# First chunk of x loaded in three pieces over two DMA queues, and recorded instruction orders in place of a greedy planner

## The chip, the cores and the metric

The kernel runs on one core of a Trainium2 chip. TensorE (PE) does the matmuls, VectorE (DVE), ScalarE (ACT) and GpSimd (POOL) the elementwise work, SyncE (SP) issues almost all DMAs. The metric is the device time of one execution in microseconds, as the median of several runs. Where the profile is used, its time is that of one profiled execution: the span runs from its first to its last instruction, and the execution's own time is a little longer.

## The reference

Two blocks read the same x (2048 tokens of 512) and are mixed by a gate per token. Cut to what matters:

```python
g = sigmoid((x * gate_w).sum(-1, keepdims=True))
# A: attention with a memory, 32 heads of 16, four segments of 512 tokens
q, k, v = x @ wq, x @ wk, x @ wv
for s in range(4):
    p = softmax(qs @ ks.T * 0.25 + causal_mask)      # inside the segment
    a_mem = (phi(qs) @ M) / (phi(qs) @ z + 1e-6)     # memory of earlier segments
    o = sigmoid(beta) * a_mem + (1 - sigmoid(beta)) * (p @ vs)
    M, z = M + phi(ks).T @ vs, z + phi(ks).sum(tokens)
a = concat(o) @ wo
# B: gated feed-forward, 1792 wide
b = (relu(x @ W_gate) * (x @ W_up)) @ W_down
out = g * a + (1 - g) * b
```

phi(t) is t + 1 where t > 0 and exp(t) elsewhere.

## The kernel before, in words

**Work.** The tokens go through in four chunks, which are also the four segments. Each chunk needs, on TensorE: the projections q, k and v (`proj`, lines 790 and 792, 48 matmuls of 128 x 128 by 512 columns); 18 *quads* of scores (`visit`, line 912), each filling four PSUM banks with 32-row matmuls that run four at a time; four *PV* products (line 968), one for each group G of eight heads, of 64 x 17 tiles; the memory update `mu` (line 835) and read-out `nd` (line 855); the feed-forward products with W_gate and W_up (`ffn`, line 1042, four matmuls for each of 28 products); and the output tiles (`outp`), which add the product with wo (line 1074, four matmuls) to that with W_down (line 1081, fourteen). Full 128-row matmuls, quads, PV and mu are different kinds of work for the array (modes f, r, h, c in the code).

ScalarE turns each quad into exponentials with one instruction over 2048 columns (line 928); GpSimd cuts the causal triangle out of them (line 934), 256 times in all; PV reads the result and VectorE transposes and scales it (lines 978 to 997). Other PSUM results are copied out by VectorE or ScalarE.

**The opening.** TensorE needs x with its features on the partitions. For chunk 0, `load` (line 618) brings x in as two halves of 256 tokens ("hT" is their buffer), SP issues both, and TensorE transposes them with an identity matrix: sixteen matmuls of 128 columns (line 706), eight evacuations called xc (line 713). Until x is there, eleven matmuls on a constant (`warm`, line 692: five of 512 columns, six of 128) keep TensorE running. Then come all four columns of Q, feature slice by feature slice, all of K, and V. Later chunks are transposed by the DMA (line 620). The three "touch" loads of 1 KB and the dummy exponential `tab` (line 645), which brings ScalarE's table load, are all that ScalarE's queue has at the start. VectorE zeroes the PSUM banks 4 to 7 (line 684), and every product that opens a bank is made to wait for that.

**What sets the order.** All work is added as `Op`s with their reads and writes. `Sched` then plays a cost model forward: at each step it takes, for each engine, the best ready head of some priority queues, with release times (`after`), bank rules and seeded jitter (`_choose`, `ready`, `_bank_choice`), and places the earliest. `place` writes the waits on semaphores and books a duration. What comes out is a fixed program for each engine: on the chip each engine goes through its list in order, and an instruction that has to wait holds up all that stand behind it on its engine, DMA issues on SP among them. Quads always use the banks 0 to 3, everything else what is free.

```python
x0 = A_x[0, 0:512, :].rearrange("(h p i) d -> h p i d", h=2, i=2)
for h in range(2):
    load("sp", [f"hT{2 * h}", f"hT{2 * h + 1}"], V.hT[:, 2 * h:2 * h + 2, :], x0[h], 1 << 18)
...
xps, xcs = [warm(5, 512, 0, 3), warm(6, 128, 0, 3)], {"dve": [], "act": []}
...
rdy = [h for h in heads if h[1] <= now + 20.0]
if rdy:
    best = min(rdy, key=lambda h: (h[0], h[1] + self.jitter(h[2])))
    return best[2], best[1]
```

Of the kernel before, what the change touches and what calls it, by code (L numbers as in the profile page):

```python
# [2 lines left out]

# [13 lines left out]
LAG = 0  # L17
PAIR = 1
LASTK = 17
HWAIT = 250.0  # L20
HEARLY = 3500.0
MWAIT = 500.0
PVR = 2
NEXT = 1150.0
TNN = 2
STRICT = 6000.0
PE_LAT = 175.0
SWITCH = 106.0
GATE_T = {0: 20000.0, 1: 44000.0, 2: 90000.0, 3: 140000.0}
UNIT_T = 400.0  # L30
X1_T = 19000.0
X2_T = 34000.0
H1_T = 14000.0
LX = 300.0
DCOST = {"ldwg0_0": 1000.0, "ldbraw": 1800.0, "ldgwb": 1300.0, "ldx1_0": 1500.0, "vsh0": 1100.0, "vsh1": 1100.0, "vsh2": 1100.0, "vsh3": 1100.0}
LAND0 = {"ldhT0": 2850.0, "ldhT2": 3100.0, "ldwq0": 3150.0, "ldwq1": 3200.0, "ldwq2": 3100.0, "ldwq3": 3000.0}
NBLK = 36
QTN, EKN, HTN, OTN, XR = 8, 4, 19, 8, 3
SBX = 0
LOW_T = {"main": 0.0, "att": 3000.0, "proj": 2000.0, "ffn": 2000.0, "mid": 3000.0, "out": 5000.0}  # L40
WIN = 8000.0
EVAC_P = 0.5
ND_P = 0.2
ADP = 1
TSP = 0
OAP = 0
UNITS = [[8] * 18] * 4
ORDER = [[(0, 1, 7, 2, 6, 3, 5, 4), (4, 0, 1, 7, 2, 6, 3, 5)] * 2] * 4
# [30 lines left out]
class Epoch:  # L79
    _n = 0  # L80

    def __init__(self, cls="mid", nb=1, at=None):
        self.nb = nb
        self.at = at
        self.group = (self,)
        Epoch._n += 1
        self.res = f"ACCep{Epoch._n}"
        self.bank = None
        self.readers = []
        self.cls = cls  # L90


class Op:
    __slots__ = ("engs", "eng", "fns", "occs", "lat", "reads", "writes", "name", "dma", "nbytes", "mode", "ep", "role",
                 "after", "nbk", "port", "base", "preds", "stream", "idx", "start", "end", "done", "cidx", "gate", "nd", "mates")

    def __init__(self, alts, reads=(), writes=(), name="", lat=0.0, dma=False, nbytes=0, mode="f", ep=None, role=None):
# [13 lines left out]
        self.after = 0.0  # L111
        self.nbk = 2
        self.port = name.startswith(PORT)
        self.base = None
        self.preds = []
        self.gate = None
        self.mates = ()
# [11 lines left out]
class Sched:  # L129
    ENGS = ("pe", "act", "dve", "pool", "sp")  # L130
    CAPS = {"ffn": 3, "proj": 2, "mid": 2, "out": 2}

    def __init__(self, ndma=16, nbanks=8, seeds=(0,)):
        self.seeds = seeds
        self.jit = {}
        self.knobs = {}
        self.low_from = False
        self.mates = ()
# [9 lines left out]
        self.queues = {e: [] for e in self.ENGS}  # L148
        self.dma_rr = 0
        self.port_free = 0.0  # L150
        self.relax = False
# [7 lines left out]
        self.busy = {e: 0.0 for e in self.ENGS}  # L159
        self.ops = []  # L160
        self.log = []
# [8 lines left out]
    def add(self, op):  # L170
# [42 lines left out]
        self.ops.append(op)  # L213
        return op

    def queue(self, prio, ops):
        by = {}
        for t in ops:
            for e in t.engs:
                by.setdefault(e, []).append(t)  # L220
        for e, ts in by.items():
            self.queues[e].append([prio, ts, 0])

    def _bank_free(self, prev, e):
        if prev is None:
            return 0.0
        return max((r.end + LAT for r in prev.readers if self.know[e][r.stream] < r.idx), default=0.0)

    def pv_due(self):
        q = self.queues["pe"][self.pvq]  # L230
        while q[2] < len(q[1]) and q[1][q[2]].done:
            q[2] += 1
        if q[2] >= len(q[1]) or q[1][q[2]].gate is None:
            return 0
        t = self.now["pe"] + 500.0
        return (PVR if q[1][q[2]].mates else q[1][q[2]].nbk) if all(p.done and p.end <= t for p, _ in q[1][q[2]].preds) else 0

    def next_visit(self):
        q = self.queues["pe"][self.attq]
        while q[2] < len(q[1]) and q[1][q[2]].done:  # L240
            q[2] += 1
        return q[1][q[2]] if q[2] < len(q[1]) else None

    def visit_in(self, dt):
        op = self.next_visit()
        if op is None:
            return False
        t = self.now["pe"] + dt
        if op.after > t or not all(p.done and p.end <= t for p, _ in op.preds):
            return False  # L250
        return all(p.done and p.end <= t + 700.0 for g in op.ep.group for rd in g.readers for p, _ in rd.preds if p.ep not in op.ep.group and p.cidx < op.cidx)

    def soon(self, dt):
        op = self.next_visit()
        if op is None or op.after - HEARLY > self.now["pe"] + dt:
            return False
        if not all(p.done and p.end + LAT <= self.now["pe"] + dt for p, _ in op.preds):
            return False
        t = max((self._bank_free(x, "pe") if x is None or all(r.done for r in x.readers) else 1e9) for x in self.bank_ep[:4])
        return t <= self.now["pe"] + dt  # L260

    def next_sides(self):
        op = self.next_visit()
        return 0 if op is None else len(op.ep.group) - 1

    def low(self, cls):
        return 0 if self.low_from and (self.relax or not self.visit_in(LOW_T[cls])) else 4

    def _bank_choice(self, ep, e, taken=()):
        cls, nb, n = ep.cls, ep.nb, len(self.bank_ep)  # L270
        idle = [i not in taken and (p is None or all(r.done for r in p.readers)) for i, p in enumerate(self.bank_ep)]
        if ep.at is not None:
            own = range(ep.at, ep.at + nb)
            return (ep.at, max(self._bank_free(self.bank_ep[i], e) for i in own)) if all(idle[i] for i in own) else None
        lo = 4 if cls == "side" else self.low(cls)
        if cls in ("proj", "ffn", "mid", "out"):
            held = sum(not f and p.cls == cls for f, p in zip(idle, self.bank_ep))
            if held + nb > (self.knob()[3] if cls == "ffn" else 2):
                return None
            free = sum(idle[lo:])  # L280
            if (free - nb < max(self.pv_due(), 1) if nb == 1 else free < (2 if self.relax else 3)):
                return None
            room = sum(idle[4:]) - (self.next_sides() if self.visit_in(self.knob()[1]) and not self.relax else 0)
        else:
            room = 8
        best = None
        for bi in range(lo, n - nb + 1):
            if not all(idle[bi:bi + nb]) or bi + nb > 4 and min(nb, bi + nb - 4) > room:
                continue
            ft = max(self._bank_free(p, e) for p in self.bank_ep[bi:bi + nb])  # L290
            key = ft + (300.0 if bi < 4 else 0.0)
            if nb == 1:
                key += 0.0 if not idle[bi ^ 1] else 200.0
            if best is None or key < best[2]:
                best = (bi, ft, key)
        return best and best[:2]

    def _banks(self, op, e):
        taken, out, t = set(), [], 0.0
        for ep in op.ep.group:  # L300
            bc = self._bank_choice(ep, e, taken)
            if bc is None:
                return None
# [11 lines left out]
    def ready(self, op, e):  # L315
        t0 = self.now[e]
        t = op.after - (HEARLY if op.mode == "r" and self.mode == "h" else 0.0)
        if op.gate is not None:
# [10 lines left out]
            if len(ft) < op.nbk:  # L329
                return None  # L330
# [871 lines left out]
```

## Time and profile before

| | us |
|---|---|
| median of 3 runs | 263.42 |
| lowest and highest of them | 262.78, 263.67 |
| the profiled execution's own time | 263.54 |
| its span | 262.3 |

| engine | busy us | share of the span |
|---|---|---|
| TensorE matmul | 255.7 | 97% |
| ScalarE | 184.5 | 70% |
| VectorE | 179.5 | 68% |
| GpSimd | 130.7 | 50% |

A busy share is a sum over instructions. Matmuls overlap in the array and the ends of single matmuls are modelled, so distances between starts tell more than durations. Some matmul records are missing: line 1042 has 432 of its 448 matmuls in the profile. In the timeline a row is a start, a length, an engine, a line, an operation with its tiles, and the number of instructions; brackets give the idle time ahead of it and what ended it. "issue" means that nothing the profile shows was waited for.

### The profile page before, as it was taken

To read this page: it belongs to the slowest core of one execution; us is meant where nothing else is said; L and a number is where in the kernel's file an instruction comes from. 1 tells how busy PE (TensorE), PEld (TensorE's weight loads), DVE (VectorE), ACT (ScalarE), POOL (GpSimd) and SP (SyncE) were. 2 spreads that over 40 slices of the span, in tenths; PEclk is the share of its full clock that TensorE was granted. 3 is DMA by queue.
4 is the path that set the end of the run, shared out by engine and by line. 5 is a ranking of instruction groups with operands and counts; after the bars stand their busy time and mean duration, and the time that the engine had idled before them with its cause. 6 is when DMAs were issued, how large, how long until landed. Compare 5 with 4: busy or idle time off the path is not lost.

```text
span 262.3 us, 6420 instructions
## 1 busy us (share of the span) xinstructions
PE 255.7 (97%) x2619; PEld 114.7 (44%) x2653; DVE 179.5 (68%) x356; ACT 184.5 (70%) x160; POOL 130.7 (50%) x295
## 2 busy tenths in 40 slices
PE   8999999999999999999999999999999999999997
PEld 5444443444344544434444544444444444444444
DVE  5488878788986577778788577757667716467600
ACT  4586689999789779785778687677777665576021
POOL 3036557564646457666645457846364454545100
PEclk9999999999999999999999999999999999999999
DMA  6999746930261135212040232010132100100011
GB/s 200 290 308 249 162 63 135 287 46 22 66 143 40 24 74 109 62 23 24 19 107 7 56 96 27 2 41 2 22 82 43 23 21 22 40 2 2 0 42 40
DMA packets 34925, 19.87 MB, mean 76 GB/s; under 512 B 24016, under 2 KB 34128, under 8 KB 34896
## 3 DMA queue, kind: packets, MB, share of 16 engines
q1 hardware_dynamic: 34800, 19.46, 31.6%
q8 instruction: 21, 0.34, 0.6%
q14 instruction: 8, 0.07, 0.1%
q10 hardware_dynamic: 96, 0.00, 0.0%
HBM read 10.40 MB, written 2.11 MB: 48 GB/s over the span
## 4 chain that ended last, share of the span: by engine, by line
PE 97%; issue 1%; DVE 1%
PE ps L1042 38%; PE ps L1081 19%; PE ps L792 11%; PE ps L912 9%; PE ps L968 6%; PE ps L790 5%; PE ps L1074 5%; PE ps L855 1%; PE ps L692 1%; PE ps L706 1%; PE ps L835 0%; DVE hT L1053 0%; DVE Tn L978 0%; DVE osb L745 0%; DVE osb L1090 0%
## 5 line engine op out<-in xcount | busy, mean ns | idle before, releaser
L934 POOL TENSOR_SCALAR_AFFINE_SELECT E<-E 64x256 bf16<-64x256 bf16 (+1 forms) x256 | 110.3, 442 | 112.2 <-ACT E L928 82.9
L928 ACT ACTIVATE E<-ps 128x2048 bf16<-128x2048 f32 x72 | 135.1, 1876 | 38.7 <-PE ps L912 38.6
L1042 PE MATMUL ps<-xT,wu 128*128 128x512 bf16 x213 | 57.2, 380 | 1.4 <-issue 1.3
L1042 PE MATMUL ps<-xT,wg 128*128 128x512 bf16 x219 | 57.7, 380 | 0.6 <-issue 0.3
L1081 PE MATMUL ps<-wd,hT 128*128 128x512 bf16 (+2 forms) x229 | 52.8, 367 | 0.9 <-issue 0.6
L1053 DVE TENSOR_TENSOR hT<-ps,rl 128x512 bf16<-128x512 f32 x56 | 38.5, 687 | 16.6 <-PE ps L1042 16.4
L1081 PEld LDWEIGHTS ps<-wd,hT 128*128 128x128 bf16 x238 | 21.4, 98 | 23.8 <-issue 2.4
L1042 PEld LDWEIGHTS ps<-xT,wg 128*128 128x128 bf16 x224 | 20.6, 98 | 25.7 <-issue 2.8
L1042 PEld LDWEIGHTS ps<-xT,wu 128*128 128x128 bf16 x224 | 20.1, 98 | 25.4 <-issue 3.5
L912 PE MATMUL ps<-qT,kp 32*128 32x192 bf16 (+7 forms) x512 | 28.6, 287 | 0.0
L978 DVE STREAM_TRANSPOSE Tn<-ps 128x512 f32<-128x512 f32 x32 | 21.3, 696 | 8.7 <-PE ps L968 8.7
L1051 DVE TENSOR_SCALAR rl<-ps 128x512 bf16<-128x512 f32 x30 | 20.7, 690 | 8.5 <-PE ps L1042 8.2
L1090 DVE TENSOR_SCALAR osb<-ps,omg 128x512 bf16<-128x512 f32 (+1 forms) x8 | 5.6, 701 | 26.0 <-PE ps L1081 15.1
L1050 ACT ACTIVATE rl<-ps 128x512 bf16<-128x512 f32 x26 | 15.5, 598 | 10.0 <-PE ps L1042 9.7
L912 PEld LDWEIGHTS ps<-qT,kp 32*128 32x128 bf16 x512 | 8.2, 92 | 25.3 <-issue 13.1
L968 PE MATMUL ps<-E,vaug 64*17 64x128 bf16 (+7 forms) x512 | 18.7, 283 | 0.0
L968 PE MATMUL ps<-E,vsh 64*17 64x128 bf16 (+7 forms) x512 | 18.3, 283 | 0.0
L1091 ACT ACTIVATE osb<-ps,omg 128x512 bf16<-128x512 f32 (+1 forms) x9 | 6.1, 674 | 16.4 <-PE ps L1074 14.0
L792 PE MATMUL ps<-xT,wq 128*128 128x512 bf16 x61 | 16.0, 390 | 0.4 <-issue 0.3
L1074 PE MATMUL ps<-wo,oT 128*128 128x512 bf16 (+2 forms) x67 | 16.2, 366 | 0.2 <-issue 0.2
L792 PE MATMUL ps<-xT,wk 128*128 128x512 bf16 x60 | 15.6, 380 | 0.4 <-issue 0.3
L968 PEld LDWEIGHTS ps<-E,vaug 64*17 64x17 bf16 x512 | 11.6, 86 | 8.5 <-issue 4.4
(68 smaller groups left out, 233.6 us busy)
## 6 DMA issues: line engine op xcount, KB each, us to landing
vsh<-vaug SPq DMA_DIRECT2D x8, 272.0 KB, 4.2
osb<-in_A_x_dram SPq DMA_DIRECT2D x16, 128.0 KB, 2.3
out_dram<-osb SPq DMA_DIRECT2D x15, 128.0 KB, 1.7
wg<-in_B_W_gate_dram SPq DMA_DIRECT2D x8, 224.0 KB, 5.7
wu<-in_B_W_up_dram SPq DMA_DIRECT2D x8, 224.0 KB, 6.2
wd<-in_B_W_down_dram SPq DMA_DIRECT2D x1, 1792.0 KB, 10.6
hT<-in_A_x_dram SPq DMA_DIRECT2D x2, 256.0 KB, 2.9
wq<-in_A_wq_dram SPq DMA_DIRECT2D x4, 128.0 KB, 3.5
```

Source lines behind the costliest of these rows:

```text
L792: ins = e.matmul(A(ep)[:, :], lhsT=w[:, kt, col * 128:(col + 1) * 128], rhs=V.xT[:, kt, tok:tok + 512], start=(kt == 0), stop=(kt == KT - 1))
L912: ins = q.matmul(dst, lhsT=V.kp[r, kslot(s, G), c, :], rhs=V.qT[r, qslot(s, G), q0:q0 + w], start=True, stop=True, tile_position=(32 * jj, ...
L928: acts.append(act(lambda a: a.activation(V.E[:, base * 512:base * 512 + min(2048, 4 * W)], PF[:, 0:min(2048, 4 * W)], ACT.Exp, scale=SCALE ...
L934: pools.append(pool(lambda g, ap=ap, lim=lim, pat=pat: g.affine_select(out=ap, in_=ap, compare_op=ALU.is_ge, fill=0.0, base=lim, pattern=[ ...
L968: ins = q.matmul(A(eps[p])[32 * jj:32 * jj + 17, 64 * (c + u):64 * (c + u + n)], lhsT=v[:, 8 * G + 2 * jj + p, :], rhs=V.E[r, f:f + 64 * n ...
L978: ds.append(dve(lambda e, p=p, ep=eps[p]: e.transpose(V.Tn[:, 2 * (G % (TNN // 2)) + p, :], A(ep)[:, :]), t_dve(512), writes=[f"Tn{2 * (G ...
L1042: ins = e.matmul(A(ep)[:, :], lhsT=w[:, kt, f * 128:(f + 1) * 128], rhs=V.xT[:, kt, c % XR * 512:(c % XR + 1) * 512], start=(kt == 0), sto ...
L1050: evs.append(sc.add(Op([("act", lambda e, ep=eg, r=r: e.activation(V.rl[:, r, :], A(ep)[:, :], ACT.Relu), t_act(512)), ("dve", lambda e, e ...
L1051: ("dve", lambda e, ep=eg, r=r: e.tensor_scalar(V.rl[:, r, :], A(ep)[:, :], 0.0, None, ALU.max), t_dve(512))],
L1053: evs.append(dve(lambda e, ep=eu, r=r, hs=hs: e.tensor_tensor(V.hT[:, hs, :], A(ep)[:, :], V.rl[:, r, :], ALU.mult), t_dve(512), reads=[f" ...
L1074: ins = e.matmul(A(ep)[:, 0:c1 - c0], lhsT=V.oT[:, ot[G], i * 128:(i + 1) * 128], rhs=V.wo[:, G, c0:c1], start=st_ and G == 0, stop=sp_ an ...
L1081: ins = e.matmul(A(ep)[:, 0:c1 - c0], lhsT=V.hT[:, slots[f], i * 128:(i + 1) * 128], rhs=V.wd[:, f, c0:c1], start=st_ and f == f0, stop=sp ...
```

## The change

1. Chunk 0 of x comes in three loads: tokens 0 to 127 ("hT0") on SP, 128 to 255 ("hT1") on ScalarE's queue, 256 to 511 ("hT2", "hT3") on SP. The sixteen transposing matmuls stay sixteen; four evacuations now cover two feature slices of 128 tokens (xca0, xca1, xcb0, xcb1), four cover one slice of 256 tokens as before (xc4 to xc7).
2. The first tile of wq is issued on ScalarE's queue too. That queue's order becomes hT1, wq0, the three touches, then the dummy exponential.
3. The second warm-up group has four matmuls in place of six. The zeroing of PSUM and the waits on it are gone.
4. Priority queues, release times, jitter and bank rules are gone. Each engine's order is a recorded list of numbers (`ORDER`), and each PSUM result's bank a digit of `BANKS`; an `Op`'s number is its place in the order in which `program` adds them. `run` and `place` remain, so that waits are worked out as before. A quad may start at any bank from 0 to 4.
5. `visit` can split quads over several visits (`SEVEN`); the lists that would ask for it are empty, so there are 72 visits of one quad, as before.
6. In the recorded order chunk 0 starts with the columns 2 and 0 of Q only, then all of K and a part of V; the columns 1 and 3 of Q come after the first quad.

The core of the diff, with the first entries of the lists:

```diff
+LAND0 = {"ldhT0": 2650.0, "ldhT1": 2750.0, "ldhT2": 3050.0, "ldwq0": 3500.0, "ldwq1": 3500.0, "ldwq2": 3400.0, "ldwq3": 3550.0, "ldwk0": 3450.0, "ldwk1": 3400.0, "ldwk2": 3350.0, "ldwk3": 3400.0,
+SEVEN = [(), (), (), ()]
+ORDER = {k: [int(x) for x in v.split()] for k, v in {
+    "pe": """
+58 59 60 62 64 66 68 70 72 74 159 134 160 135 161 162 136 137 149 139 174 140 164 150 175 165 190 196 191 193 385 194 144 391 145 392 386 202 187 146
...
+    "act": """
+5 7 0 1 2 3 63 67 71 75 151 154 197 179 395 203 148 76 209 186 215 413 189 221 227 425 238 341 244 335 90 250 336 256 344 351 449 273 354 279 360 285
...
+    "sp": """
+4 6 8 9 10 11 12 13 14 15 16 17 18 19 20 21 22 23 24 25 26 28 29 39 27 82 84 43 30 158 38 86 32 36 40 37 88 201 200 31 34 33 95 183 45 182 35 157 97
...
     def run(self):
+        for ep in self.eps:
+            if ep.at is None:
+                ep.bank = int(self.banks[ep.idx])
...
+        todo = {e: [self.ops[i] for i in self.order[e]] for e in self.ENGS}
...
-    x0 = A_x[0, 0:512, :].rearrange("(h p i) d -> h p i d", h=2, i=2)
-    for h in range(2):
-        load("sp", [f"hT{2 * h}", f"hT{2 * h + 1}"], V.hT[:, 2 * h:2 * h + 2, :], x0[h], 1 << 18)
+    for n, w in enumerate((W_g, W_u, W_d)):
+        load("act", [f"touch{n}"], V.adT[0:16, 32 * n:32 * n + 32], w[0:16, 0:32], 1024)
+    act(lambda e: e.activation(V.eb[:, 0:8], nc.const_aps.tensor(1.0, [128, 8], BF16), ACT.Exp), 100, writes=["eb"], name="tab")
+    load("sp", ["hT0"], V.hT[:, 0, :], A_x[0, 0:128, :], 1 << 17)
+    load("act", ["hT1"], V.hT[:, 1, :], A_x[0, 128:256, :], 1 << 17)
+    load("sp", ["hT2", "hT3"], V.hT[:, 2:4, :], A_x[0, 256:512, :].rearrange("(p i) d -> p i d", i=2), 1 << 18)
...
-            load(eng, [f"{nm}{kt}"], w[:, kt, :], src[kt * 128:(kt + 1) * 128, :], 1 << 17)
+            load("act" if (nm, kt) == ("wq", 0) else eng, [f"{nm}{kt}"], w[:, kt, :], src[kt * 128:(kt + 1) * 128, :], 1 << 17)
...
-    for b in range(4):
-        ds.append(dve(lambda e, b=b: e.memset(PS[:, 4 + b, :], 0.0), 500, writes=[f"init{b}"], name=f"init{b}"))
...
+    for m, n, role in ((5, 512, "w"), (4, 128, "w2")):
```

In these numbers 0 to 2 are the touches, 3 is `tab`, 4 to 6 the loads of x, 7 to 18 those of wq, wk and wv, 58 and 59 the warm-ups, 60 to 75 transposes and evacuations by turns, 134 to 195 the projections of chunk 0 (134 to 137 column 0 of Q, 159 to 162 column 2), and 196 the first quad.

More of the change, by code (lines that the diff above doesn't have):

```diff
@@ L213, in add @@
         self.ops.append(op)
-        return op
[L216 to L296, printed above, removed]
```

710 lines of the change are left out of this document (235 added, 475 removed), and 35 rows, old and new, of the table ORDER.

## The prediction

> **What bounds the kernel now.** First the page: how busy each engine is, and what the chain that ended last consists of.
>
> ```profile
> span 262.3 us, 6420 instructions
> ...
> PE 255.7 (97%) x2619; PEld 114.7 (44%) x2653; DVE 179.5 (68%) x356; ACT 184.5 (70%) x160; POOL 130.7 (50%) x295
> ...
> PE 97%; issue 1%; DVE 1%
> ```
>
> The chain is TensorE from end to end. A busy share alone does not say that nothing is lost between the matmuls, so the second view is TensorE's waits after its first transpose, window 3.8 to 260.4 (us in total, times, longest):
>
> ```profile
> PE ps L1042 <- issue: 1.6, 10, 0.2
> PE ps L1081 <- issue: 0.6, 4, 0.2
> PE ps L792 <- issue: 0.6, 4, 0.2
> PE ps L1074 <- issue: 0.2, 1, 0.2
> PE ps L1042 <- DVE Tn L978: 0.2, 1, 0.2
> ```
>
> 3.2 us in twenty pieces, none over 0.2. The third view, TensorE's timeline, says what such a piece is:
>
> ```profile
> 15.57 0.40 PE L912 MATMUL ps<-qT,kp 32*128 32x448 bf16 x8
> 15.90 1.47 PE L790 MATMUL ps<-wv,xT 128*128 128x512 bf16 x6
> ...
> 18.07 1.03 PE L1042 MATMUL ps<-xT,wu 128*128 128x512 bf16 x4
> 19.03 0.40 PE L912 MATMUL ps<-qT,kp 32*128 32x384 bf16 x8
> 19.59 0.81 PE L1042 MATMUL ps<-xT,wg 128*128 128x512 bf16 x3 [0.16 <-issue]
> 20.23 1.03 PE L1042 MATMUL ps<-xT,wu 128*128 128x512 bf16 x4
> ```
>
> Three matmuls from 19.59 to 20.23 are 0.214 us each. The quad (scores, L912) at 15.57 is followed after 0.33 us, the one at 19.03 after 0.56; but L1042 issues four matmuls per product, and only three are recorded. The "wait" is one unrecorded matmul (0.33 + 0.21). Four matmuls from 18.07 fill 0.86 of 0.96 us: entering a quad costs 0.10. So TensorE has no hole that a better order could fill; an order can change only how often it changes kind of work, the opening, and the end.
>
> The fourth view is the opening's timeline:
>
> ```profile
> 0.80 1.28 ACT L645 ACT_TABLE_LOAD   x1 [0.80 <-PEq L1187]
> 0.81 0.86 SPq L618 DMA_DIRECT2D hT<-in_A_x_dram  x2
> 0.84 2.93 PE L692 MATMUL ps<-const-bfloat16-1.0 128*128 128x512 bf16 x11 [0.84 <-PEq L1187]
> 0.87 0.39 ACTq L618 DMA_DIRECT2D adT<-in_B_W_gate_dram  x1
> 1.72 1.85 SPq L618 DMA_DIRECT2D wq<-in_A_wq_dram  x4
> 2.10 0.21 ACT L645 ACTIVATE eb<-const-bfloat16-1.0 128x8 f32<-128x8 bf16 x1
> 3.61 1.86 SPq L618 DMA_DIRECT2D wk<-in_A_wk_dram  x4
> 3.74 1.63 PEld L706 LDWEIGHTS ps<-ident,hT 128*128 128x128 bf16 x16 [0.23 <-DMA hT<-in_A_x_dram]
> 5.42 4.17 PE L792 MATMUL ps<-xT,wq 128*128 128x512 bf16 x16
> 5.85 0.15 PEld L792 LDWEIGHTS ps<-xT,wq 128*128 128x128 bf16 x1 [0.28 <-issue]
> 6.28 0.15 PEld L792 LDWEIGHTS ps<-xT,wq 128*128 128x128 bf16 x1 [0.28 <-issue]
> 6.63 2.47 PEld L792 LDWEIGHTS ps<-xT,wq 128*128 128x128 bf16 x12 [0.20 <-issue]
> 7.41 1.86 SPq L618 DMA_DIRECT2D wg<-in_B_W_gate_dram  x4
> ```
>
> Eleven warm-up matmuls cover the wait for x; the transposes start at 3.74, when x has landed, and Q at 5.42. The first Q matmuls come 0.43 us apart, the rest 0.21: TensorE runs at half pace until about 6.5 us, though the granted clock reads 1.00 all along.
>
> **The change, part by part.**
>
> *First chunk of x.* What the start waits for is the landing:
>
> ```profile
> vsh<-vaug SPq DMA_DIRECT2D x8, 272.0 KB, 4.2
> osb<-in_A_x_dram SPq DMA_DIRECT2D x16, 128.0 KB, 2.3
> ...
> hT<-in_A_x_dram SPq DMA_DIRECT2D x2, 256.0 KB, 2.9
> wq<-in_A_wq_dram SPq DMA_DIRECT2D x4, 128.0 KB, 3.5
> wk<-in_A_wk_dram SPq DMA_DIRECT2D x4, 128.0 KB, 3.2
> ```
>
> Today 0.81 + 2.9 = 3.71. The new first load has half the bytes. If it lands no sooner, the gain is 0. The quiet 128 KB row (2.3) would land it at 3.11, but the warm-ups end later: five of 512 columns at 0.43 and four of 128 at a quarter of that, 2.57 us from 0.84, so 3.41, and 3.74 - 3.41 = 0.33 is the most to be gained. I take the middle, 0.17: transposes from 3.57, Q from 3.57 + (5.42 - 3.74) = 5.25. The second slice (ACT, about 0.87 + 2.9 = 3.77) is wanted after four transposes at 3.57 + 4 x 0.105 = 3.99 (sixteen take 5.42 - 3.74), the 256 KB rest (SP, 1.24 + 2.9 = 4.14) after eight, at 4.41; cover 0.2 to 0.3.
>
> What is the earlier start worth? At half pace until 6.5, 0.17 us does half its work: 0.09. If the pace changed earlier by as much, all 0.17. I take 0.09, since the first warm-up still starts at 0.84.
>
> [...]
>
> *ScalarE's queue.* The groups by line give the evacuations of the transposes, and the PSUM memsets used below:
>
> ```profile
> L684 DVE MEMSET ps<- 128x512 f32 x4 | 1.9, 485 | 1.2 <-PEq L1187 1.0
> L713 DVE CAST xT<-ps 128x256 bf16<-128x256 f32 x4 | 1.5, 420 | 1.2 <-PE ps L706 1.2
> L713 ACT ACTIVATE xT<-ps 128x256 bf16<-128x256 f32 x4 | 1.4, 382 | 2.3 <-PE ps L706 2.3
> ```
>
> Five DMA issues now precede the dummy exponential; at SP's 0.43 each (0.86 for two) they end at 0.87 + 5 x 0.43 = 3.02. If the table load (1.28) waits for them, ScalarE is free at 3.02 + 1.28 + 0.21 = 4.51 instead of 2.31. Behind it stand four copies of 0.38: xca1, xcb1, xc5, xc7, done at 4.89, 5.27, 5.65 and 6.03. Q now does columns 2 and 0 alone, so each slice of x is used after two matmuls instead of four: the second at 5.25 + 0.86 = 6.11 (needs xc5: cover 0.4), the last slice near 7.0 (needs xc7: 0.9). Cost 0; if the cover fails, each 0.1 of lateness costs 0.1, or half before 6.5.
>
> *Weights.* wq0 goes to ACT, and SP issues all that follows 0.47 us earlier (a fourth of 1.86), so K's deadline moves against its loads. Eight Q matmuls, three of them slow, end at 5.25 + 3 x 0.43 + 5 x 0.216 = 7.6 (today, by the same count, sixteen end at 9.5). wk0 and wk1 are issued at 3.14 and 3.6 and land 3.2 later, 6.8; wk2, wk3 by 7.8, wanted after three half products at 8.9. Eight K halves (3.45) and one V half bring the first quad to about 11.6. The first wg product comes at about 12.8, where its loads matter:
>
> ```profile
> wg<-in_B_W_gate_dram SPq DMA_DIRECT2D x2, 224.0 KB, 4.2
> ```
>
> The first two issued at 7.41 and 7.9 land at 11.6 and 12.1 today, at or before that after the change: cover 0.7 at least. Cost 0.
>
> *Further down SP's queue* one placed wait matters: the vsh copies wait for the last V copy, ScalarE's vcp0_1, which the table puts behind exp0_0_3 and a relu, by my count of its products near 25 us. Behind them on SP stand wg1_2, wu1_1, wu1_0. At 4.2 us for vsh the shifted values land at 29.3; the table puts the first PV near 32. The next user, wg0_7, is near 35. Cost 0.
>
> *PSUM.* Four VectorE memsets (485 ns each) go from the very start; VectorE's first copies had to wait 1.2 us for the transposes all the same. Worth 0. Quads may now stand at banks 0 to 4; the exponential reads four banks in one piece as before. Cost 0.
>
> *Orders.* Counted in program() order, the "pe" table holds the same products, 72 quads, 16 PV and 3 mu, with two warm-ups less. Its changes of kind number 164, 60 of them from full matmuls into a quad. The before timeline also has 164 and 60. At 0.10 each, a difference of 0. With no wait to remove, all reordering after 12 us is worth 0 at best; a misplaced entry costs its lateness.
>
> *End.* The table keeps the last 128 columns' fourteen matmuls, the wo product, VectorE's copy and the 32 KB store last. Cost 0.
>
> Sum: -0.09 against the profiled 263.54 (span 262.3 and 1.2 around it), which lies 0.12 above the median: 263.42 - 0.09 = 263.33, say **263.3**.
>
> **The rivals.**
>
> *No earlier landing* (two queues share engines): 263.4. For it, loads in company land late: 128 KB of wq take 3.5 us, 256 KB of x ahead of them 2.9. Against it, the first slice is issued 0.06 ahead of the second.
>
> *Full pace sooner.* The change of pace at 6.5 falls on no event of the program. If it comes up to 2.7 us sooner, at the first transpose, up to 2.72/2 = 1.4 is saved: 262.0 to 263; I price it at 262.4. The three runs of before spread over 0.9 us, which would fit such a shift between runs; nothing shows that the change causes it. [...]
>
> *Slower: a hole ahead of the transposes.* Warm-ups now end at 3.41 against 3.63 today. If x lands at 3.57 to 3.74, TensorE idles 0.2 to 0.3, today 0.1. If the half-pace stretch, 6.5 - 0.84 = 5.7 us from the first matmul, starts anew there, it lasts to 3.57 + 5.7 = 9.3, and 2.8 us more at half pace cost 1.4: 264.7. It decides from the point where a hole of 0.2, not 0.1, counts as idleness. Against it: small holes are common in any opening.
>
> *Slower by the tables.* Replayed orders cannot step aside: if one quad in ten of the 72 waits 0.15 us, they lose 7 x 0.15 = 1.1: 264.4. Against it: before's program is as fixed once built, and never waits.
>
> **How the numbers follow.** Forecast 0.55, no earlier landing 0.15, full pace sooner 0.14, hole 0.09, tables 0.07. A measurement of this kernel tells 0.3%, 0.8 us, from no change: faster means under 262.6, slower over 264.2. Faster 0.14, same 0.70, slower 0.16. The range must leave out 0.2: the slower cases (0.16) and the outer part of full pace sooner, so 262.2 to 263.9; the unknown landing (0 to 0.33) and the opening's cover lie inside.
>
> **What would show it.** Right: transposes at 3.45 to 3.7, first quad near 11.6, no TensorE wait over 0.2 after that, the last matmul about as long before the end. Wrong: Q rows 0.43 apart beyond 7 us (hole), under three slow ones (full pace sooner), a wait on ACT's xT copies or on a wg load (cover gone), or quads with real gaps ahead of them (tables).

## The result, and the profile after

The changed kernel takes 264.34 us (median of 7 runs, 263.90 to 264.92) against 263.22 for the kernel before in the same measurement (7 runs, 262.78 to 263.67): ratio 1.0047, interval 1.0032 to 1.0063. It is slower by 1.1 us, where 0.1 us less was forecast. Of the kernels tried further down, pad_both_wq0_late had one execution, the profiled one, at a mean granted clock of 0.987 (268.88 us); it is left out of that kernel's median, and its columns in the table are empty.

The page of the changed kernel's profile (its own time 264.91, span 263.3) shows TensorE busy as before, and a chain that is no longer TensorE alone:

```profile
span 263.3 us, 6429 instructions
PE 259.1 (98%) x2651; PEld 113.7 (43%) x2651; DVE 173.9 (66%) x346; ACT 187.0 (71%) x166; POOL 120.6 (46%) x295
...
PE 94%; DMA 3%; DVE 1%; SPq 0%; issue 0%
```

TensorE's waits between 3.3 and 260 us (in total, times, longest) name three places; none of them is among the waits of before:

```profile
PE ps L852 <- DVE oT L763: 0.5, 1, 0.5
PE ps L523 <- DMA hT<-in_A_x_dram: 0.4, 1, 0.4
PE ps L583 <- DVE xT L507: 0.2, 1, 0.2
```

Two of them lie in the opening. TensorE's rows of the timeline:

```profile
3.55 1.04 PE L514 MATMUL ps<-ident,hT 128*128 128x128 bf16 x8
4.97 0.62 PE L523 MATMUL ps<-ident,hT 128*128 128x128 bf16 x8 [0.39 <-DMA hT<-in_A_x_dram]
5.77 1.90 PE L583 MATMUL ps<-xT,wq 128*128 128x512 bf16 x8 [0.18 <-DVE xT L507]
7.51 3.62 PE L583 MATMUL ps<-xT,wk 128*128 128x512 bf16 x16
10.96 0.59 PE L581 MATMUL ps<-wv,xT 128*128 128x512 bf16 x2
11.49 0.39 PE L696 MATMUL ps<-qT,kp 32*128 32x512 bf16 x4
```

The transposes start at 3.55 and the first quad at 11.49 (it was 12.55), both as forecast. In between stands a hole that was not: the second eight transposes wait for the third piece of x until 4.97. That piece was issued in the SP group that starts at 0.81, behind the first, so at about 1.24; it took 3.7 us. What paid for the hole is the pace: the eight Q matmuls from 5.77 to 7.51 go at 0.22 us each, so the full pace was there at 5.8 and not at 6.5.

The third place is the first product with wo, at 82.75. The rows that lead to it, in the timeline of all engines:

```profile
75.84 3.06 SPq L543 DMA_DIRECT2D osb<-in_A_x_dram  x1
...
81.37 0.69 DVE L544 CUSTOM_DVE_ANT_0 osb<-osb,gwb 128x512 bf16<-128x512 bf16 x1 [1.82 <-DMA osb<-in_A_x_dram]
...
81.98 0.71 DVE L763 STREAM_TRANSPOSE oT<-adT 128x512 bf16<-128x512 bf16 x1
...
82.75 0.82 PE L852 MATMUL ps<-wo,oT 128*128 128x512 bf16 x3 [0.47 <-DVE oT L763]
```

A tile of x for the gate, issued at 75.84, keeps SP for 3.06 us and lands 5.5 us after its issue; VectorE stands idle 1.82 us for it, though the transpose of oT behind it in VectorE's list needs nothing from it; TensorE then waits for oT. In the same stretch lies a 16 KB packet of kind "instruction" on a queue of its own, q8, which took 2.93 us from 75.7 on (this trace's others take 0.9 to 1.4). The trace has 21 of these to TensorE's 5302 matmuls and weight loads, one to about 250; from that they are taken here for fetches of TensorE's program, and the 8 KB packets of the same kind on q14 for those of the other engines. From 75.5 to 79 us the packet is 5.2% of the 16 DMA engines' time, which is one engine for 2.93 us:

```profile
q8 instruction: 1, 0.02, 5.2%
...
osb<-in_A_x_dram SPq DMA_DIRECT2D x1, 128.0 KB, 5.5
```

Last, the end: first before's timeline and its DMA view of the window 261 to 263.4 (packets, MB and the share of 16 engines; then the issues, with the time to landing), then the same of the changed kernel.

```profile
260.02 0.39 PE L1074 MATMUL ps<-wo,oT 128*128 128x128 bf16 x4
260.05 1.11 SPq L1093 DMA_DIRECT2D out_dram<-osb  x2
260.45 0.35 DVE L1090 TENSOR_SCALAR osb<-ps,omg 128x128 bf16<-128x128 f32 x1 [10.86 <-PE ps L1074]
```

```profile
q1 hardware_dynamic: 249, 0.10, 15.3%
...
out_dram<-osb SPq DMA_DIRECT2D x1, 32.0 KB, 1.5
```

```profile
260.55 0.39 PE L852 MATMUL ps<-wo,oT 128*128 128x128 bf16 x4
260.69 1.00 SPq L870 DMA_DIRECT2D out_dram<-osb  x2
260.97 0.35 DVE L867 TENSOR_SCALAR osb<-ps,omg 128x128 bf16<-128x128 f32 x1 [1.88 <-PE ps L852]
```

```profile
q1 hardware_dynamic: 288, 0.13, 19.0%
q14 instruction: 1, 0.01, 1.8%
...
out_dram<-osb SPq DMA_DIRECT2D x1, 32.0 KB, 1.9
```

From the last product's start to the end of the span it is 262.3 - 260.02 = 2.28 us before and 263.3 - 260.55 = 2.75 after. The copy and the issue take the same; the last store lands 0.4 later. New in that window is the row "q14 instruction", one packet of 8 KB. It starts at 261.68, right behind the last store's issue, and takes 0.67 us. A store leaves 16 increments of its semaphore in the trace as it lands. Of the last store's, fifteen have come by 262.80 and the sixteenth at 263.28, 0.48 later; in before all sixteen lie between 262.11 and 262.28. This fits a fetch that holds one of the 16 DMA engines, so that the part of the store that goes over it comes last.

So the profiled 264.91 - 263.54 = 1.37 us splits into three: the last product starts 260.55 - 260.02 = 0.53 later, the tail behind it is 0.47 longer, and the time outside the span goes from 263.54 - 262.3 = 1.24 to 264.91 - 263.3 = 1.61, 0.37 more. The prediction had looked for a difference in the first of these only. The first is the difference of two single executions: before's profiled one lies 0.32 above before's median.

### The profile page after: what moved, and what is told of

The parts are those of the page before. It is cut to its first block, busy times and chain, and to the rows that moved or that the text cites. A ratio compares the mean times of both kernels' runs of the same rounds, so it can differ in the third digit from the quotient of the medians.

```text
span 263.3 us, 6429 instructions
## 1 busy us (share of the span) xinstructions
PE 259.1 (98%) x2651; PEld 113.7 (43%) x2651; DVE 173.9 (66%) x346; ACT 187.0 (71%) x166; POOL 120.6 (46%) x295
## 4 chain that ended last, share of the span: by engine, by line
PE 94%; DMA 3%; DVE 1%; SPq 0%; issue 0%
PE ps L822 37%; PE ps L859 19%; PE ps L583 11%; PE ps L696 9%; PE ps L743 7%; PE ps L852 5%; PE ps L581 5%; DMA osb<-in_A_x_dram 2%; DMA hT<-in_A_x_dram 1%; PE ps L639 1%; PE ps L622 1%; DVE osb L544 0%; DVE oT L763 0%; DVE xT L507 0%; SPq L448 0%; DVE osb L867 0%
## 5 line engine op out<-in xcount | busy, mean ns | idle before, releaser
L713 POOL TENSOR_SCALAR_AFFINE_SELECT E<-E 128x256 bf16<-128x256 bf16 (+1 forms) x256 | 100.8, 421 | 102.2 <-ACT E L706 91.8
L822 PE MATMUL ps<-xT,wu 128*128 128x512 bf16 x224 | 60.8, 380 | 0.0
L822 PE MATMUL ps<-xT,wg 128*128 128x512 bf16 x224 | 60.1, 380 | 0.0
L859 PE MATMUL ps<-wd,hT 128*128 128x512 bf16 (+2 forms) x238 | 56.8, 367 | 0.0
L831 DVE TENSOR_SCALAR rl<-ps 128x512 bf16<-128x512 f32 x33 | 22.6, 686 | 11.7 <-PE ps L822 11.5
L760 POOL TENSOR_TENSOR adT<-Tn,rdg 128x512 bf16<-128x512 f32 x12 | 12.7, 1055 | 20.3 <-DVE rdg L758 18.6
L867 DVE TENSOR_SCALAR osb<-ps,omg 128x512 bf16<-128x512 f32 (+1 forms) x12 | 8.6, 714 | 15.3 <-PE ps L859 8.7
L583 PE MATMUL ps<-xT,wq 128*128 128x512 bf16 x64 | 17.8, 380 | 0.2 <-DVE xT L507 0.2
L581 PE MATMUL ps<-wv,xT 128*128 128x512 bf16 x64 | 17.3, 380 | 0.0
L830 ACT ACTIVATE rl<-ps 128x512 bf16<-128x512 f32 x23 | 13.6, 595 | 5.0 <-PE ps L822 4.1
```

What stands on the lines that cost most here:

```text
L581: ins = e.matmul(A(ep)[:, :], lhsT=V.xT[:, kt, tok + col * 128:tok + (col + 1) * 128], rhs=w[:, kt, :], start=(kt == 0), stop=(kt == KT - 1))
L583: ins = e.matmul(A(ep)[:, :], lhsT=w[:, kt, col * 128:(col + 1) * 128], rhs=V.xT[:, kt, tok:tok + 512], start=(kt == 0), stop=(kt == KT - 1))
L713: pool(lambda g, ap=ap, lim=lim: g.affine_select(out=ap, in_=ap, compare_op=ALU.is_ge, fill=0.0, base=lim, pattern=[[0, 4], [1, 64]], chan ...
L822: ins = e.matmul(A(ep)[:, :], lhsT=w[:, kt, f * 128:(f + 1) * 128], rhs=V.xT[:, kt, c % XR * 512:(c % XR + 1) * 512], start=(kt == 0), sto ...
L831: ("dve", lambda e, ep=eg, r=r: e.tensor_scalar(V.rl[:, r, :], A(ep)[:, :], 0.0, None, ALU.max), t_dve(512))],
L859: ins = e.matmul(A(ep)[:, 0:c1 - c0], lhsT=V.hT[:, slots[f], i * 128:(i + 1) * 128], rhs=V.wd[:, f, c0:c1], start=st_ and f == f0, stop=sp ...
```

## The experiments

Medians and ratios are against runs of the kernel before on the same chip: 263.15 for the first four kernels, 263.38 for the next four, 263.31 for the four after them, 263.33 for the last three. Of each profiled execution the table has the first quad's start, the last product's start, the stretch between them, the tail (span less the last product's start), and the time outside the span. Spans are shown to 0.1 us, so the last two columns are good to 0.05.

| kernel | median us | ratio, interval | first quad | last product | stretch | tail | outside |
|---|---|---|---|---|---|---|---|
| before | 263.22 | | 12.55 | 260.02 | 247.47 | 2.28 | 1.24 |
| after | 264.34 | 1.0047 (1.0032 to 1.0063) | 11.49 | 260.55 | 249.06 | 2.75 | 1.61 |
| again | 264.24 | 1.0035 (1.0021 to 1.0048) | 11.45 | 259.89 | 248.44 | 2.81 | 1.54 |
| wq0_on_sp | 264.69 | 1.0055 (1.0042 to 1.0069) | 11.65 | 260.16 | 248.51 | 3.44 | 1.54 |
| gate9_after_bt | 263.83 | 1.0027 (1.0012 to 1.0042) | 13.47 | 261.88 | 248.41 | 2.62 | 1.30 |
| two_halves | 263.94 | 1.0029 (1.0019 to 1.0039) | 11.67 | 260.09 | 248.42 | 2.31 | 1.55 |
| after_pad | 263.86 | 1.0017 (1.0008 to 1.0026) | 11.55 | 260.30 | 248.75 | 2.30 | 1.56 |
| before_pad15 | 263.43 | 1.0003 (0.9993 to 1.0012) | 11.69 | 259.38 | 247.69 | 2.72 | 1.22 |
| before_pad40 | 263.26 | 0.9996 (0.9987 to 1.0005) | 11.96 | 259.82 | 247.86 | 2.28 | 1.25 |
| pad_wq0_gate9 | 263.67 | 1.0006 (0.9995 to 1.0016) | 11.72 | 260.14 | 248.42 | 2.26 | 1.24 |
| after_pad_both | 263.61 | 1.0011 (0.9997 to 1.0025) | 11.09 | 260.17 | 249.08 | 2.23 | 1.27 |
| before_pool99 | 263.99 | 1.0026 (1.0017 to 1.0036) | 12.52 | 259.99 | 247.47 | 2.31 | 1.54 |
| after_pad_wq0 | 263.93 | 1.0028 (1.0017 to 1.0039) | 11.68 | 260.09 | 248.41 | 2.31 | 1.53 |
| after_pad_both_wq0 | 264.05 | 1.0032 (1.0018 to 1.0045) | 12.18 | 260.59 | 248.41 | 2.31 | 1.18 |
| pad_gate9 | 263.38 | 1.0008 (0.9995 to 1.0022) | 11.45 | 259.87 | 248.42 | 2.23 | 1.26 |
| pad_gate9_wq0_late | 264.59 | 1.0067 (1.0044 to 1.0089) | 12.43 | 260.85 | 248.42 | 2.25 | 1.26 |
| pad_both_wq0_late | 264.93 | 1.0070 (1.0049 to 1.0090) | | | | | |

The stretch of before isn't comparable with that of after, since after has done less of Q by the first quad.

### The parts of the change

**again** is the changed kernel once more.

> The changed kernel once more, for a second trace. If the waits in its first profile are part of the program (x's third piece late by 0.7 us; 0.63 us ahead of the first wo product near 82 us, behind a gate row that landed after 5.5 us; 0.5 us more between TensorE's end and the end of the last store), all of them show again within 0.2 us and the time is 264.3, 1.004 of before. If they are accidents of one execution, at least one is gone from this profile.

It repeats 1.0035, the hole (0.44 and 0.16 us), the longer tail and the longer time outside the span; TensorE doesn't wait at 82 us. Its last product starts 0.13 *before* that of before, and the execution is still 264.24 - 263.54 = 0.70 longer than before's profiled one. Between these two executions the loss lies wholly behind TensorE's last product.

**wq0_on_sp** puts the first tile of wq back on SP's queue.

```diff
-5 7 0 1 2 3 63 67 71 ...
+5 0 1 2 3 63 67 71 ...
-4 6 8 9 10 11 ...
+4 6 7 8 9 10 11 ...
-load("act" if (nm, kt) == ("wq", 0) else eng, [f"{nm}{kt}"], ...
+load(eng, [f"{nm}{kt}"], ...
```

> Only the first tile of wq goes back from ScalarE's queue to SP's, in its old place behind x. Theory (packets of the two queues alternate, so wq0 on the second queue holds up x's third piece): the third piece lands near 4.2 instead of 4.9, the hole of 0.6 us among the transposes goes, Q starts near 5.2, and the time falls by 0.4 to 0.8 us. Rival (the third piece is late for itself, with three loads of x in flight): the third piece still lands at 4.7 or later and the time stays within 0.2.

The third piece of x now lands at 4.22, and the hole among the transposes is gone. A wait for the next tiles of wq takes its place:

```profile
4.30 1.08 PE L523 MATMUL ps<-ident,hT 128*128 128x128 bf16 x8
5.24 1.19 PE L583 MATMUL ps<-xT,wq 128*128 128x512 bf16 x4
6.68 1.16 PE L583 MATMUL ps<-xT,wq 128*128 128x512 bf16 x4 [0.26 <-DMA wq<-in_A_wq_dram]
7.67 3.62 PE L583 MATMUL ps<-xT,wk 128*128 128x512 bf16 x16
```

K starts at 7.67 against 7.51. So wq0 on ScalarE's queue did delay x by 0.7 us (4.92 to 4.22), and taking it away regains nothing: SP issues the other tiles one step later. The tail is 3.44: here the last store lands 2.6 us after its issue, with the q14 packet beside it (fifteen increments by 262.41, the sixteenth at 263.55).

**gate9_after_bt** swaps two neighbours of VectorE's list, the gate's product that waits for its tile and the transpose of oT behind it.

```diff
-... 481 749 111 483 722 ...
+... 481 749 483 111 722 ...
```

> One pair swapped in VectorE's recorded order: the gate's row 9 behind the transpose that makes oT for G=3 of segment 0, everything else as in the changed kernel. Theory (the order puts a transfer that can be late ahead of work that TensorE waits for): the wait of 0.63 us ahead of the first wo product near 82 us goes, and the time falls by 0.3 to 0.6 us. Rival (that row's lateness was an accident of one execution): no wait there in this profile either way, and the time stays within 0.15.

It takes 263.83 us, and TensorE doesn't wait at 82 us. Of the 0.4 us that its median lies below again's, about 0.3 is time outside the span (1.30), which no expectation had. The profiled execution is the slowest of the twelve (265.8; the others 263.50 to 264.24), and has the late full pace of the prediction's rival "hole":

```profile
3.60 1.03 PE L514 MATMUL ps<-ident,hT 128*128 128x128 bf16 x8
5.12 1.03 PE L523 MATMUL ps<-ident,hT 128*128 128x128 bf16 x8 [0.48 <-DMA hT<-in_A_x_dram]
6.03 3.59 PE L583 MATMUL ps<-xT,wq 128*128 128x512 bf16 x8
9.42 3.69 PE L583 MATMUL ps<-xT,wk 128*128 128x512 bf16 x16
```

Eight Q matmuls take 3.39 us, 0.42 each: half pace until 9.4, though the granted clock reads 1.000. The price is the first quad at 13.47, 2 us late.

**two_halves** loads x as before does (two loads of 256 tokens, wq0 on SP) and keeps the tables.

```diff
-load("sp", ["hT0"], V.hT[:, 0, :], A_x[0, 0:128, :], 1 << 17)
-load("act", ["hT1"], V.hT[:, 1, :], A_x[0, 128:256, :], 1 << 17)
+load("sp", ["hT0", "hT1"], V.hT[:, 0:2, :], A_x[0, 0:256, :].rearrange("(p i) d -> p i d", i=2), 1 << 18)
```

> The changed kernel's tables with the old loads: x in two halves of 256 tokens, both and wq0 on SP, ScalarE's queue left with the touches and the dummy exponential. If the opening is what costs, the transposes start at 3.75, run without a hole, Q starts near 5.4, and the time is 0.3 to 0.8 us below the changed kernel. If the new opening is a gain or nothing and the recorded orders are what costs, the time is the changed kernel's or 0.1 to 0.3 above it.

1.0029: the tables without the new loads are slower too. The tail is 2.31 here (the fetch comes after the end of the span, at 263.6), the time outside 1.55. The median is 0.3 below that of again, as the expectation had it for an opening that costs, but the tail alone is 0.5 shorter, so this gain doesn't speak for the opening.

### The lengths of the programs

ScalarE's program has 176 instructions before and 191 after (the new load's issue, the tables' choice of engine for copies), GpSimd's 346 and 317. These lengths are one more than the instructions in the trace; the expectations give ScalarE's without that one. Of the eight fetches of 8 KB on q14 inside the span, seven in before and seven in after fall where some engine's count of recorded instructions stands within 12 of 64, 192 or 320: in before at 72.70 us with ScalarE at its 61st instruction, at 128.82 with GpSimd at its 192nd, at 212.35 with GpSimd at its 308th, the last one. In after, ScalarE reaches its 190th at the end of the kernel: the fetch at 261.68. Theory: a longer ScalarE program moves a fetch onto the last stores. Rival: something in the change's stores.

**after_pad** puts 12 waits that are long fulfilled into ScalarE's program (203 instructions), so that the fetch comes earlier.

```diff
+extra = 12 if e == "act" else 0
+for at, item in enumerate(prog):
+    if extra and at > 40 and at % 9 == 0:
+        engobj.wait_ge(self.sem["pool"], 1)
+        engobj.wait_ge(self.sem["pe"], 1)
+        extra -= 1
```

> The changed kernel with twelve waits that are already fulfilled spread over ScalarE's program (190 instructions become 202). In its traces an 8 KB instruction fetch falls 0.3 to 0.8 us behind the issue of the last store and holds one DMA engine for 0.6 to 1.1 us; in before the last such fetch is at 212 us, and ScalarE's program has 175 instructions there. Theory (ScalarE's program now ends at a place where the next block is fetched): with 202 the fetch falls some 20 us before the end, the time from the last matmul's start to the span's end goes from 2.6 back to 2.1, the time outside the span from 1.58 towards 1.24, and the kernel is 0.5 to 0.8 us faster than the changed one. Rival (the tail is the stores' own, of their new order): tail 2.6 and time stay, or the time rises by the 0.7 us of the waits.

Twelve instructions that do nothing make the kernel faster: 1.0017 against 1.0035 to 1.0047 (its interval ends at 1.0026; after's begins at 1.0032, again's at 1.0021). The fetch has gone to 206.65, and the end is as long as before's, 2.30 us; the time outside the span, which the theory also had shrink, stayed at 1.56. The DMA view of the window 261 to 263.4 has no q14 row, the last store lands in 1.4, and its sixteen increments come within 0.2 us (262.37 to 262.55):

```profile
q1 hardware_dynamic: 288, 0.13, 19.1%
...
out_dram<-osb SPq DMA_DIRECT2D x1, 32.0 KB, 1.4
```

**before_pad15** and **before_pad40** do the same to the kernel before: 15 waits (191, as in after) and 40 (216).

> The kernel before with fifteen waits that are already fulfilled spread over ScalarE's program, so that it has 190 instructions as the changed kernel has; orders, loads and tables of before. Theory of the fetch: a fetch of 8 KB appears behind the last store, the tail grows from 2.1 to 2.6 and the time outside the span by 0.3, so 264.0, 0.8 us above before, without any of the change. Rivals (stores, opening, tables): the time stays within 0.2 of before.

> The control: before with forty such waits (215 instructions). Theory of the fetch: the fetch falls well before the end, tail 2.1, and the time is that of before within 0.2, below that with fifteen waits. If it is the waits themselves that cost, it is slower than with fifteen.

With 191 the fetch appears at 260.74 and the tail is 2.72, with 216 the fetch is at 180.16 and the tail 2.28. The DMA view of before_pad15 from 260.4 on:

```profile
q1 hardware_dynamic: 237, 0.09, 10.4%
q14 instruction: 1, 0.01, 0.6%
...
out_dram<-osb SPq DMA_DIRECT2D x1, 32.0 KB, 1.9
```

Fifteen increments of its last store are there by 261.65, the sixteenth at 262.06. The median of before_pad15 didn't rise all the same (1.0003). In its profile TensorE had its full pace from about 4 us and its last product started 0.64 sooner than in before's, which hides the tail in that one execution; for the other eleven no trace tells why. So a longer tail beside a fetch is shown in both kernels, its price in the median only in the changed one.

**pad_wq0_gate9** joins after_pad, wq0_on_sp and gate9_after_bt.

> The changed kernel with all three suspected costs taken away: twelve waits on ScalarE (201 instructions), wq0 back on SP, VectorE's gate row 9 behind oT. If the three are all that the change costs, it is at before or up to 0.3 us below: 262.9 to 263.2. If the fetch alone matters, it equals the changed kernel with the waits, within 0.2.

1.0006: the changed kernel stands level with before. Unexpected was the time outside the span, 1.24. It was 1.5 to 1.6 in all changed kernels but those with the gate swapped. The swap also shortens GpSimd's program, which needs two waits less, from 317 to 315: a second program near a fetch. The next four tell length from swap.

**after_pad_both** has 12 such waits on GpSimd too (329), **before_pool99** puts 99 into before's (445 = 317 + 128), **after_pad_wq0** and **after_pad_both_wq0** are wq0_on_sp with the first or both sets.

```diff
-extra = 12 if e == "act" else 0
+extra = 12 if e in ("act", "pool") else 0
```

> The changed kernel with 12 waits, each already fulfilled, on ScalarE (as in after_pad) and 12 more on GpSimd; nothing left out. Theory 'GpSimd's program ends at a block': the 0.33 us more outside the span (1.24 in before, 1.5 to 1.6 in after, again, after_pad) belong to kernels whose GpSimd program is 317 instructions long; 315 and 346 don't have them. With 329 the time outside the span is 1.24 and the median 0.3 under after_pad: about 263.5, ratio to before 1.0005. Rival 'the gate's place': the 0.33 went away in two kernels because the gate stands behind the copy, and length has nothing to do with it: outside stays 1.55 to 1.6, median 263.9, ratio 1.0017.

> The kernel before with 99 fulfilled waits on GpSimd, so that its program has 445 instructions, which is 317 + 128; nothing left out. Theory 'GpSimd's program ends at a block of 128': the time outside the span goes from 1.24 to 1.55 or 1.6, the median by 0.33: ratio 1.0012. Rivals: only 317 matters, or it is another property of the changed kernel: outside 1.24, ratio 1.000. If the 99 waits themselves cost GpSimd time, the exponentials' mask comes later and TensorE would show waits on it; GpSimd is busy half of the span, so none is expected.

> after_pad with wq0 back on SP's queue, the gate's place unchanged; nothing left out. Theory of the opening: the third piece of x lands at about 4.2 instead of 4.9, the hole among the transposes (0.6 to 0.7) goes, holes of 0.3 to 0.5 inside Q take its place since SP now issues wq1 to wq3 later: worth 0 to 0.3, median 263.5 to 263.9; outside the span stays 1.55 to 1.6 (GpSimd 317). Rival: the whole of the hole is regained, 263.2.

> after_pad_wq0 with the 12 waits on GpSimd as well; nothing left out. By 'GpSimd's program ends at a block' it is 0.33 below after_pad_wq0 and equals the kernel with both repairs and the gate behind the copy (ratio 1.0006): 1.000 to 1.0006, outside 1.24. Rival: the gate's place was worth 0.3 by itself, and this one stays at 1.0015 to 1.002.

The time outside the span follows GpSimd's length, in both kernels and whatever the order: 1.53 to 1.61 with 317 (six kernels), 1.54 with 445; 1.18 and 1.27 with 329, 1.24 to 1.30 with 315 (four), 1.22 to 1.25 with 346 (three). This is no accident of the profiled executions: every run has its time and its span on record, and their difference is 1.52 to 1.64 in every execution of the seven kernels with 317 or 445, and 1.17 to 1.31 in every other. In after_pad_both a fetch that the kernels with 317 don't show has moved into the span, to 233.93. The median of before_pool99 rose by more than the 0.3 of the theory (1.0026); its profile has 0.3 more than before's, all of it outside the span; what the rest of its median is stays open. What happens outside the span isn't in the trace; that it is the fetch is inferred from the lengths.

wq0 on SP was no gain either way: 1.0028 against after_pad's 1.0017, 1.0032 against after_pad_both's 1.0011.

### What was left

**pad_gate9** has ScalarE's 12 waits and the swap, with the change's own opening. **pad_gate9_wq0_late** issues wq0 behind the three touches, **pad_both_wq0_late** does so without the swap, with both sets of waits.

```diff
-5 7 0 1 2 3 63 67 71 ...
+5 0 1 2 7 3 63 67 71 ...
```

> The changed kernel with the 12 fulfilled waits on ScalarE and the gate's exponent behind the copy bt0_3 on VectorE (which also makes GpSimd's program 315 long); the opening is the change's own, with wq0 on ScalarE's queue. Nothing left out. Theory 'blocks and the stall at 82': tail 2.10, outside 1.24, no stall at 82, only the hole among the transposes left: ratio 1.000 to 1.0005 (263.3). Rival 'opening': the hole of 0.4 to 0.7 is a loss that nothing pays back, 1.0015 to 1.002. Rival 'the gate's place is worth nothing': the same as after_pad_both, 1.0011.

> pad_gate9 with wq0 behind the three touches on ScalarE's queue, so that it is issued some 1.3 us later, at about 2.6. Nothing left out. Theory: the third piece of x then has the DMA engines nearly to itself and lands at 4.2 instead of 4.9, the hole among the transposes goes; wq0 lands near 4.9 and Q starts at 5.2: 0.3 to 0.6 below pad_gate9 if TensorE's full pace comes as early as there, near 262.9, ratio 0.998 to 0.999. Rival: Q then waits for wq0 or for the copies instead, as in wq0_on_sp: no difference.

> The same late wq0 with the gate's place as in the change, and the 12 waits on ScalarE and on GpSimd. Nothing left out. Against pad_gate9_wq0_late it shows what the gate's place costs once the program's length is out of it: 0.0 to 0.2 if the stall at 82 comes in some executions only, 0.4 to 0.7 if the difference between pad_wq0_gate9 (1.0006) and after_pad_both_wq0 (1.0032) was the gate's.

pad_gate9 comes to 263.38, 0.05 above before's median: no difference that these runs tell, with a hole of 0.57 us among its transposes. Twelve idle instructions and one swap take back 1.0 of the 1.1 us. The late wq0 makes it worse, against the theory: issued at 2.66 behind SP's loads, it took 4.0 us and landed at 6.7, not at 4.9. The row of the DMA issues, and the only wait that TensorE's view names:

```profile
wq<-in_A_wq_dram ACTq DMA_DIRECT2D x1, 128.0 KB, 4.0
```

```profile
PE ps L588 <- DMA wq<-in_A_wq_dram: 1.2, 1, 1.2
```

A wait of 1.2 us there moved the median by 264.59 - 263.38 = 1.2: what the opening loses after its transposes reaches the end in full. pad_both_wq0_late comes to 1.0070 against 1.0067, so with the late opening the gate's place makes no difference that these runs tell. That losses pass through is also what the column "stretch" says: from the first quad to the last product it is 248.41 to 248.44 in eight of the changed kernels' twelve profiles (248.51 in a ninth), whatever the opening was. Only three are longer, those in which the wo product at 82 us waits: after by 0.64, after_pad by 0.33, after_pad_both by 0.66. These are among the five whose first quad came before 11.6; the two others are again, where oT was ready just in time, and pad_gate9, where the swap took the gate's product out of oT's way. None of the four with the swap waits there. So what an early opening gains can be given back at 82 us, because VectorE stands behind a DMA. The late tile itself belongs to the recorded order: in all twelve profiles SP is held 2.4 to 3.4 us at that issue, and a 16 KB fetch beside it takes 2.5 to 3.1, against 1.0 to 1.4 for the fetch at 74 to 75 us in the four profiles of before. How often this happens in runs without a profile, and so its share of the median, stays open: pad_gate9 and after_pad_both differ by 0.23 us, within their intervals, pad_wq0_gate9 and after_pad_both_wq0 by 0.38, outside theirs, though the latter's profile has no wait there. No version here beats the kernel before.

## Why the prediction was wrong, point by point

- **"End: cost 0" failed.** The order of the last work was as it said, and its cost was read off that order. What it missed was the instructions' own traffic: the changed programs end beside a fetch. ScalarE's costs 0.47 us in the tail (2.28 to 2.75; after_pad brings 2.30), GpSimd's about 0.3 outside the span (1.24 to 1.61; after_pad_both brings 1.27). Together 0.8 of the 1.1 us. The first is seen in the traces and taken away by idle instructions; that the second is a fetch is inferred. after_pad_both, which has neither, is still 0.3 above before (1.0011, whose interval includes 1).
- **"All reordering after 12 us is worth 0 at best; a misplaced entry costs its lateness" was right, and the entry was there.** The rival "tables" had it as many small waits on quads; it was one wait of 0.3 to 0.7 us at one place, in three of the changed kernels' profiles. That the changes of kind were worth nothing, as forecast, isn't contradicted: from the start of Q at full pace to the last product it is 254.14 us in pad_gate9 (5.73 to 259.87) and 254.27 in before_pad15 (5.11 to 259.38).
- **The first load: right, the 0.17 by luck.** Transposes at 3.55, forecast 3.57; TensorE idle ahead of them 0.25 us (0.23 before). The forecast was the middle between two bounds, and the load's 2.7 us happened to lie there. The rival "no earlier landing" didn't come: the first slice landed at about 3.5, the second (2.9 us) at 3.7.
- **"Cover 0.2 to 0.3" for the third piece failed.** It was priced at 2.9 us and took 3.7; the deadline, 4.41, came at about 4.3. The prediction let the two queues compete for the first two slices (its rival "no earlier landing"), not for the third piece with wq0 behind hT1 on ScalarE's queue. wq0_on_sp shows it: 4.22 without it. In after's trace 223 packets of SP's queue (q1) and 222 of ScalarE's (q10) start from 2.5 to 4.0 us, with 64.8% and 39.1% of the 16 DMA engines' time: together they fill it (a packet that runs past 4.0 counts whole).
- **The sum of the opening, -0.09, looks right only beside before's profiled execution.** The last product starts 0.13 (again) and 0.15 us (pad_gate9) before the one there: its transposes have a hole of 0.44 and 0.57 us, but the full pace came before Q instead of at 6.5. In before's two profiles with the full pace ahead of Q (before_pad15, before_pad40) the last product starts at 259.38 and 259.82, sooner than again's 259.89 and pad_gate9's 259.87. So at like pace the opening gained nothing. An estimate, from each median less the profile's tail and time outside, puts the last product at 263.22 - 2.28 - 1.24 = 259.70 before and 264.34 - 2.75 - 1.61 = 259.98 after: about the 0.3 that is left of the 1.1. Whether the hole or the wait at 82 us makes it, the runs don't tell.
- **"Full pace sooner": its condition came, not its time.** It came before Q, or with Q's first matmul, in nine of the changed kernels' twelve profiles (at about 6.3 in after_pad_both_wq0, 6.5 in pad_wq0_gate9, 9.4 in gate9_after_bt) and in two of four of before's (first quad at 11.69 and 11.96, against 12.55 and 12.52). It comes and goes in either kernel; whether the change makes it likelier, so few can't tell, and what sets it off no run shows.
- **"Hole ahead of the transposes": it exists, one place later, and seldom.** One execution (gate9_after_bt, 265.8) kept half pace until 9.42, the 9.3 of the prediction's sum. Holes of nearly that size in after_pad, after and pad_gate9 (0.70, 0.65 and 0.57, here 0.74, by the weight loads) didn't bring it about. So a hole of 0.70 is not sufficient, and whether the one of 0.74 was the cause isn't shown.
- **Weights, ScalarE's copies, vsh, PSUM: cost 0 held**, but for 0.2 us that Q waits for a copy of the late third piece.
- **The range.** Its upper end, 263.9, left out slower cases for which the prediction had no term: whatever lies between TensorE's last product and the end of the run was taken from before as a constant, "1.2 around it". Its starting point, the 263.42 of three runs, also lay 0.2 above the 263.22 of seven.

## What to carry to other kernels

Compare the stretch behind the bounding engine's last instruction, and the time outside the span, as two terms of their own: here they held about 0.8 of 1.1 us while TensorE's own work hardly differed. Where a change adds or removes instructions, look also at where the fetches fall: here twelve waits on ScalarE moved one from 261.68 to 206.65 us, and fifteen in before brought one to 260.74. If one falls on the last store, a few idle instructions on that engine are a cheap test, and were a repair here (tail 2.75 to 2.30). And in a list replayed in order, look behind each instruction that waits for a DMA for one that TensorE will need: here, swapping the two cost nothing that the runs tell (pad_gate9 1.0008, after_pad_both 1.0011).

## What the runs showed of the hardware

- The traces list packets of kind "instruction" among those whose time the page counts as a share of the 16 DMA engines: 8 KB on q14 (eight in the span, 0.3 to 1.3 us each in before and after) and 16 KB on q8 (21, 0.9 to 2.9 us), one to about 250 of TensorE's matmuls and weight loads. On q14 the fetches that fit VectorE's count in before lie 131 and 123 of its instructions apart (at its 61st, 192nd and 315th). Where one met the last store, the tail was 0.47 us longer (after).
- The same fetch costs by its moment: 0.3 to 1.2 us of tail, against before's 2.28, in the five profiles where it lies on the last stores (261.68 in after, 261.76 in wq0_on_sp, where the tail is 3.44), nothing in the tail where it comes after the landing (two_halves).
- A DMA issue can hold SP 3.06 us (75.84) where the next of the same line takes 0.34; a 16 KB fetch of 2.93 us lay beside it. The pair recurs in all twelve profiles of the changed kernels. That the one caused the other wasn't tried; two DMA transposes issued just ahead (72.54 and 74.65) are another candidate for both.
